# A decode kernel that reads 290 MB: rounds of two heads on halves of the partitions, with wider rows for V and the first weights

## The chip, the cores and the metric

The kernel runs on one core of one Trainium2 chip. The metric is the device time of one execution in microseconds, as the median of the runs shown. Each matmul in float32 shows as two passes on PE in the trace, each with its own weight load.

## The reference

Two rows of activations (batch B = 2, one token each, D = 448) pass through two branches, which a gate mixes:

```python
# x: (2, 1, 448); k_cache, v_cache: (2, 16, 4096, 256), all float32
g = sigmoid((x * gate_w).sum(-1, keepdims=True))
q = (x @ wq).reshape(B, Sq, 16, 256).transpose(0, 2, 1, 3)
p = softmax(einsum("bhqd,bhkd->bhqk", q, k_cache) * 256 ** -0.5)
a = einsum("bhqk,bhkd->bhqd", p, v_cache).transpose(0, 2, 1, 3).reshape(B, Sq, 4096) @ wo
h = x @ w1 + b1                      # (2, 1, 1792)
b = where(h > 0, h, 0) ** 2 @ w2 + b2
out = g * a + (1 - g) * b
```

K and V are 134 MB each; the weights wq, wo, w1 and w2 together are 21 MB. All of it is read once.

## The kernel before

**Layout.** The work goes by pairs of batch and head, 32 in all, in the order of the heads with the two batches in turn. For a pair, the 4096 keys lie on 128 partitions with 32 keys each, so that K and V are each one tile of 128 x 32 KB (4 MB, `slot`). All large tiles (K, V, wq in two, w1, w2's first two rows, w2's rest, and four groups of wo) share one pool with five slots of 32 KB per partition, the ring. A tile takes a slot when it is first written and gives it back after its last reader.

**Order.** The order of the instructions on each engine is the order in which the program writes them (`manual_schedule`). SP's queue issues all loads of the ring. An issue that waits for a slot holds up all later issues on that queue.

**One pair on the engines.** DVE multiplies K by q in place (`times_q`, L294), in three pieces of 4, 12 and 16 keys per partition for all pairs but the first. It then sums each key's 256 products (`row_sums`, L300), and takes the largest score of each partition (`maximum`, L304). PE spreads these maxima over the partitions (L306), DVE takes the largest of them with its sign changed (`softmax`, L312), and ACT writes the exponentials into a zeroed weight tile `pw` and their sums into `rs` (L317). PE multiplies the exponentials with V (`values`, L343): two keys per partition and matmul, 16 matmuls of 512 columns, in 32 passes, into four row groups of a PSUM bank. While PE and ACT do this, DVE is already at the next pair: the first 4 keys are multiplied before the exponential, the next 12 after it, and the rest in `rest`.

**Units of heads.** Four heads (two batches each) form a unit with one PSUM accumulator. When a unit is done, DVE forms the factors 1/sum times the gate (`norm`, three instructions), ACT copies the accumulator (`take`, L354), PE turns it (`turn`, L372, 16 matmuls) and multiplies it with the unit's part of wo (`project`, L385). The last four heads form units of three and one, and are projected with separate small matmuls (`late_wo`, `late_w2`, L390).

**The rest.** q for all heads is computed at the start (`project_q`, L228) from wq in two ring tiles, and is spread over the partitions for two heads at a time (`make_q`, L239). The dense branch is put in the first pairs: `load_w1` with pair 2, `ffn_hidden` and `ffn_turn` with pairs 3 and 4, the loads of w2's first two rows with pair 4, `ffn_square` (four small DVE instructions) at its end. Loads of K and V of a pair stand at L139, the loads of w2's rest at L111, of wo at L125 (units 0 to 2) and L128 (the last heads). The last pair's V is cut into pieces of 2, 1 and 1 MB; behind it, w2's rest comes in four pieces.

The last loads and the end are, in the order of the program: V of the last pair but one with wo of the last heads between its halves, V of the last pair, w2's rest; then values, the turn of the last unit, the late matmuls, one copy by ACT (L500) and two small stores.

Of the kernel before, what the change touches and what calls it, by code (L numbers as in the profile page):

```python
# [8 lines left out]
F32 = mybir.dt.float32  # L9
# [7 lines left out]
def kernel(  # L17
# [14 lines left out]
    nc = tc.nc  # L32
# [5 lines left out]
    CF = D // P  # L38
    R0 = CF * P
    RR = D - R0  # L40
    assert 2 * RR == P and B == 2 and CF == 3
    NK = S // P
    J = 32
    NCH = NK // J
# [7 lines left out]
    QH = QB // DH  # L52
    DQ = D // 4
    RING = 5
    WH = 2
    W2_CUTS = (4, 8, 11)
    LEAD = 4
# [4 lines left out]
    ring = ctx.enter_context(tc.tile_pool(name="ring", bufs=RING))  # L62
# [8 lines left out]


    wq_t = []

    def load_wq():

        ta = slot("wqa")
        nc.sync.dma_start(ta, wq[:2 * P, :].rearrange("(p c) n -> p (c n)", c=2))
# [3 lines left out]
        wq_t.extend([ta[:, :N], ta[:, N:], tb_[:, :N], tb_[:, N:N + N // 2]])  # L82

    w1_t = []

    def load_w1():
        t = slot("w1")
        nc.sync.dma_start(t[:, :2 * F], w1[:2 * P, :].rearrange("(p c) n -> p (c n)", c=2))
        nc.sync.dma_start(t[:, 2 * F:3 * F], w1[2 * P:R0, :])
        nc.sync.dma_start(t[:, 3 * F:3 * F + F // 2], w1[R0:, :].rearrange("r (s n) -> (r s) n", s=2))  # L90
        w1_t.extend([t[:, :F], t[:, F:2 * F], t[:, 2 * F:3 * F], t[:, 3 * F:3 * F + F // 2]])
# [39 lines left out]
    def load_kv(src, i, nm, cuts=(), between=None):  # L131
        b, h = pairs[i]
        v = src[b, h].rearrange("(n p j) d -> n p j d", p=P, j=J)
        tiles = []
        for n in range(NCH):
            t = slot(f"{nm}{b}_{h}_{n}").rearrange("p (j d) -> p j d", d=DH)
            at = [0, *(cuts if n == NCH - 1 else ()), J]
            for lo, hi in zip(at, at[1:]):
                nc.sync.dma_start(t[:, lo:hi, :], v[n, :, lo:hi, :])  # L139
                if between is not None and hi < J:  # L140
                    between()
            tiles.append(t)
        return tiles

    pairs = [(b, h) for h in range(H) for b in range(B)]
    last = len(pairs) - 1


    load_wq()
# [21 lines left out]
    units = [list(range(g * HG, (g + 1) * HG)) for g in range(NG - 1)] + [list(range(H - HG, H - 1)), [H - 1]]  # L171
    unit_of = {h: (u, k) for u, hs in enumerate(units) for k, h in enumerate(hs)}

    pw = {}
    for k in range(HG):
        for b in range(B):
            pw[k, b] = const.tile([P, NK // 2, 4 * HG], F32, name=f"pw{k}_{b}")
            nc.vector.memset(pw[k, b], 0.0)

# [6 lines left out]
    xr2 = const.tile([B, RR, 2], F32, name="xr2")  # L186
    nc.vector.tensor_copy(xr2, x2[:, R0:].unsqueeze(2).to_broadcast([B, RR, 2]))
    pxt = ps.tile([P, 512], F32, name="pxt", tag="sm")
    pxv = pxt[:, :(CF + 1) * B].rearrange("p (c b) -> p c b", b=B)
    for c in range(CF + 1):  # L190
        src = (x2[:, c:2 * P:2] if c < 2 else x2[:, c * P:(c + 1) * P] if c < CF
               else xr2.rearrange("b r s -> b (r s)"))
        nc.tensor.matmul(pxv[:, c, :], src, ident[:B, :B], start=True, stop=True)
    xT = const.tile([P, CF + 2, B], F32, name="xT")
    nc.vector.tensor_copy(xT[:, :CF, :], pxv[:, :CF, :])
    for s in range(2):
        nc.vector.tensor_scalar(xT[:, CF + s, :], pxv[:, CF, :], eo[:, s:s + 1], None, op0=ALU.mult)
# [19 lines left out]
    qs = const.tile([P, NQ // 4, QB], F32, name="qs")  # L217

    def project_q():
        for c in range(CF + 1):  # L220
            for n in range(NQ):
                a, gq = divmod(n, 4)
                if c < CF:
                    lt, rhs = xT[:, c, :], wq_t[c][:, n * QB:(n + 1) * QB]
                else:
                    half, m = divmod(n, NQ // 2)
                    lt, rhs = xT[:, CF + half, :], wq_t[c][:, m * QB:(m + 1) * QB]
                nc.tensor.matmul(po_bufs[a][32 * gq:32 * gq + B, :], lt, rhs, start=(c == 0), stop=(c == CF))  # L228
        for a in range(NQ // 4):
            nc.scalar.activation(qs[:, a, :], po_bufs[a], AF.Copy, scale=scale)  # L230
# [3 lines left out]
    def make_q(b, n):  # L234

        a, gq = divmod(n, 4)
        r = 32 * gq + b
        pq = ps.tile([P, 512], F32, name=f"pq{b}_{n}", tag="pq")
        nc.tensor.matmul(pq, ident[:, r:r + 1].to_broadcast([P, P]), qs[:, a, :], start=True, stop=True)  # L239
        t = work.tile([P, QB], F32, name=f"q{b}_{n}", tag=f"q{b}")  # L240
        nc.scalar.activation(t, pq, AF.Copy)  # L241
        for k in range(QH):
            q_sb[b, n * QH + k] = t[:, k * DH:(k + 1) * DH]
# [6 lines left out]
    h_sb = shared[:B, :F]  # L250

    def ffn_hidden():
        ph = ps.tile([P, 512], F32, name="ph", tag="pq")
        for c in range(CF + 1):
            for n in range(FB):
                if c < CF:
                    lt, rhs = xT[:, c, :], w1_t[c][:, n * D:(n + 1) * D]
                else:
                    half, m = divmod(n, FB // 2)
                    lt, rhs = xT[:, CF + half, :], w1_t[c][:, m * D:(m + 1) * D]  # L260
                nc.tensor.matmul(ph[32 * n:32 * n + B, :D], lt, rhs, start=(c == 0), stop=(c == CF))
        for n in range(FB):
            nc.scalar.activation(h_sb[:, n * D:(n + 1) * D], ph[32 * n:32 * n + B, :D], AF.Copy)

    def ffn_turn():
        hv = h_sb.rearrange("b (p c) -> b c p", c=FC)
        pt = ps.tile([P, FC, B], F32, name="pt", tag="sm")
        for c in range(FC):
            nc.tensor.matmul(pt[:, c, :], hv[:, c, :], ident[:B, :B], start=True, stop=True)  # L269
        return pt  # L270

    def ffn_square(pt):
        hb = const.tile([P, FC, B], F32, name="hb")
        nc.vector.tensor_tensor(hb, pt, b1T.unsqueeze(2).to_broadcast([P, FC, B]), op=ALU.add)
# [5 lines left out]
    kts, s_t, rs_t, rl_t, oT = {}, {}, {}, {}, {}  # L280

    def parts(lo, hi):

        while lo < hi:
            e = min(hi, (lo // J + 1) * J)
            yield lo // J, lo % J, lo % J + e - lo
            lo = e

    def times_q(i, lo, hi):

        b, h = pairs[i]
        for n, a, e in parts(lo, hi):
            kt = kts[i][n][:, a:e, :]
            nc.vector.tensor_tensor(kt, kt, q_sb[b, h].unsqueeze(1).to_broadcast([P, e - a, DH]), op=ALU.mult)  # L294

    def row_sums(i, lo, hi):
        if lo == 0:
            s_t[i] = work.tile([P, NK], F32, name=f"s{i}", tag="s")
        for n, a, e in parts(lo, hi):
            nc.vector.tensor_reduce(s_t[i][:, n * J + a:n * J + e], kts[i][n][:, a:e, :], axis=AX.X, op=ALU.add)  # L300

    def maximum(i):
# [3 lines left out]
        nc.tensor.matmul(mt[:, :P], m.to_broadcast([P, P]), ident, start=True, stop=True)  # L306
        return mt

    def softmax(i, mt):
        b, h = pairs[i]  # L310
        nb = work.tile([P, 1], F32, name=f"nb{i}", tag="nb")
        nc.vector.tensor_reduce(nb, mt[:, :P], axis=AX.X, op=ALU.max, negate=True)  # L312
        u, k = unit_of[h]
        c = B * k + b
        if c == 0:
            rs_t[u] = work.tile([P, B * len(units[u])], F32, name=f"rs{u}", tag="rs")
        nc.scalar.activation(pw[k, b][:, :, 2 * c:2 * c + 2], s_t[i].rearrange("p (m s) -> p m s", s=2), AF.Exp,  # L317
                             bias=nb, accum_out=rs_t[u][:, c:c + 1])

    def sums(u):  # L320
        sm = ps.tile([P, 512], F32, name=f"sum{u}", tag="sm")
        nc.tensor.matmul(sm[:, :B * len(units[u])], ones_pp, rs_t[u], start=True, stop=True)  # L322
# [12 lines left out]
    def values(i, vt, lo=0, hi=NK // 2):  # L335
        b, h = pairs[i]
        u, k = unit_of[h]
        n = len(units[u])
        po = po_bufs[u % 2]
        for m in range(lo, hi):  # L340
            r = 32 * (m % 4)
            j = 2 * m
            nc.tensor.matmul(po[r:r + 4 * n, :], pw[k, b][:, m, :4 * n],  # L343
                             vt[j // J][:, j % J:j % J + 2, :].rearrange("p j d -> p (j d)"),
                             start=(k == 0 and b == 0 and m < 4), stop=(k == n - 1 and b == B - 1 and m >= NK // 2 - 4))
# [56 lines left out]
    kts[0] = load_kv(k_cache, 0, "k")  # L402
    project_q()
    make_q(0, 0)
    make_q(1, 0)
    for n in range(NCH):
        times_q(0, n * J, (n + 1) * J)
# [123 lines left out]
```

## Time and profile before

| | us |
|---|---|
| median of 3 runs | 683.41 (683.37 to 683.63) |
| the profiled execution, device time | 683.23 |
| its span, first to last instruction | 681.4 |
| DVE busy | 581.1 |
| PE busy (matmuls) | 296.5 |
| ACT busy | 37.9 |

In the rows of the profile, a timeline line has the start, the duration, the engine, the line of the program, the operation, the output and inputs, shapes, and how many instructions were merged; in brackets stands how long the engine was idle before and what ended that. "SPq" is the issuing of a load by SP, not its transfer. In a table of stages each row has the stretch, its length, the busy time and the number of instructions of PE, PE's weight loads, DVE, ACT and GpSimd, then the granted clock of PE, the mean busy share of the 16 DMA engines and GB/s. Rows on DMA issues have the count, the size of each in KB and the median time from issue to landing.

### The profile page before, as it was taken

What the parts mean: (1) busy time and instruction counts of PE and PEld (TensorE: products, weight loads), DVE (VectorE), ACT (ScalarE), POOL (GpSimd) and SP (SyncE); (2) the same over time, 40 slices, a digit from 0 to 9 for tenths busy, and PEclk for the clock granted to TensorE, in tenths of its full rate; (3) what the DMA queues carried; (4) which work ended last, traced back from release to release, by engine and by line L of the source; (5) the groups of instructions that cost most, each with busy time, mean ns of one, the idle gap of its engine ahead of it and who ended that gap; (6) DMA issues with size and microseconds to landing.
All of it is one profiled execution on the core that took longest, in us unless ns stands there. A gap on an engine that the chain in (4) does not pass through costs nothing.

```text
span 681.4 us, 3865 instructions
## 1 busy us (share of the span) xinstructions
PE 296.5 (44%) x1598; PEld 96.8 (14%) x1598; DVE 581.1 (85%) x233; ACT 37.9 (6%) x113; POOL 0.7 (0%) x6
## 2 busy tenths in 40 slices
PE   4413445543359134433347543422455712443066
PEld 1000111400115001000014110000112200101013
DVE  3299997989896999999996999899997899999990
ACT  0200001000010000000001000000001000000000
POOL 0000000000000000000000000000000000000000
PEclk9856667787656776665667865567667757667579
DMA  8999999999999999999999999999999999999996
GB/s 370 435 433 435 430 425 431 426 434 436 431 437 430 431 431 431 430 431 431 432 426 441 431 431 432 433 429 431 431 430 423 432 431 431 430 435 437 423 419 270
DMA packets 12380, 289.79 MB, mean 425 GB/s; under 512 B 1478, under 2 KB 1612, under 8 KB 2892
## 3 DMA queue, kind: packets, MB, share of 16 engines
q1 hardware_dynamic: 12200, 289.55, 99.1%
q8 instruction: 12, 0.20, 0.1%
q10 hardware_dynamic: 164, 0.02, 0.0%
q14 instruction: 4, 0.03, 0.0%
HBM read 289.56 MB, written 0.00 MB: 425 GB/s over the span
## 4 chain that ended last, share of the span: by engine, by line
DMA 59%; DVE 37%; PE 2%; issue 0%; SPq 0%; ACT 0%; DVEq 0%; ACTq 0%
DMA k<-in_A_k_cache_dram 56%; DVE k L294 18%; DVE s L300 18%; DMA w<-in_B_w_dram 3%; PE acc L385 1%; PE po_buf L343 1%; DVE nb L312 0%; PE mt L306 0%; DVE m L304 0%; PE fin L390 0%; SPq L111 0%; ACT oT L378 0%; SPq L81 0%; ACT pw L317 0%; SPq L80 0%
## 5 line engine op out<-in xcount | busy, mean ns | idle before, releaser
L294 DVE TENSOR_TENSOR k<-k,q 128x3072 f32<-128x3072 f32 (+3 forms) x94 | 285.1, 3057 | 75.7 <-DMA k<-in_A_k_cache_dram 75.7
L300 DVE TENSOR_REDUCE s<-k 128x32 f32<-128x8192 f32 x32 | 278.0, 8686 | 2.2
L343 PE MATMUL po_buf<-v,pw 128*16 128x512 f32 (+2 forms) x1024 | 181.1, 857 | 218.3 <-DMA v<-in_A_v_cache_dram 217.4
L343 PEld LDWEIGHTS po_buf<-v,pw 128*16 128x16 f32 (+2 forms) x1024 | 36.7, 123 | 349.8 <-issue 319.7
L306 PE MATMUL mt<-ident,m 128*128 128x128 f32 x64 | 19.1, 389 | 136.2 <-DVE m L304 136.2
L317 ACT ACTIVATE pw<-s,nb 128x32 f32<-128x32 f32 x32 | 10.3, 323 | 544.0 <-DVE nb L312 544.0
L306 PEld LDWEIGHTS mt<-ident,m 128*128 128x128 f32 x64 | 11.9, 233 | 167.7 <-DVE m L304 117.1
L385 PE MATMUL acc<-wo,oT 128*2 128x448 f32 x48 | 22.9, 640 | 4.9 <-ACT oT L378 4.9
L239 PE MATMUL pq<-qs,ident 128*128 128x512 f32 x32 | 24.6, 868 | 0.0
L372 PEld LDWEIGHTS ot<-rl,shared 128*128 128x128 f32 x96 | 18.8, 304 | 0.0
L372 PE MATMUL ot<-rl,shared 128*128 128x8 f32 x96 | 18.8, 338 | 0.0
L312 DVE TENSOR_REDUCE nb<-mt 128x1 f32<-128x128 f32 x32 | 9.1, 284 | 1.7 <-PE mt L306 1.7
L241 ACT ACTIVATE q<-pq 128x512 f32<-128x512 f32 x16 | 9.4, 588 | 9.5 <-PE pq L239 9.5
L322 PE MATMUL sum<-rs,ones_pp 128*128 128x8 f32 (+2 forms) x10 | 2.8, 349 | 11.3 <-ACT pw L317 11.3
L354 ACT ACTIVATE shared<-po_buf 128x1024 f32<-128x1024 f32 x6 | 5.8, 1020 | 30.9 <-PE po_buf L343 30.9
L385 PEld LDWEIGHTS acc<-wo,oT 128*2 128x2 f32 x48 | 4.3, 94 | 21.3 <-issue 16.2
L239 PEld LDWEIGHTS pq<-qs,ident 128*128 128x128 f32 x32 | 6.9, 262 | 1.3 <-ACT qs L230 0.9
L269 PE MATMUL pt<-ident,shared 2*128 2x2 f32 x28 | 7.0, 378 | 0.0
L269 PEld LDWEIGHTS pt<-ident,shared 2*128 2x128 f32 x28 | 6.9, 336 | 0.1
L304 DVE TENSOR_REDUCE m<-s 128x1 f32<-128x32 f32 x32 | 5.9, 186 | 1.1
L317 ACT ACTIVATION_READ_ACCUMULATOR pw<-s,nb 128x1 f32 x32 | 6.0, 187 | 0.0
L228 PE MATMUL po_buf<-wqa,xT 128*2 128x512 f32 x32 | 5.6, 858 | 0.8 <-DMA wqa<-in_A_wq_dram 0.8
(62 smaller groups left out, 55.3 us busy)
## 6 DMA issues: line engine op xcount, KB each, us to landing
k<-in_A_k_cache_dram SPq DMA_DIRECT2D x32, 4096.0 KB, 40.0
v<-in_A_v_cache_dram SPq DMA_DIRECT2D x30, 4096.0 KB, 31.6
wo<-in_A_wo_dram SPq DMA_DIRECT2D x4, 1792.0 KB, 34.1
v<-in_A_v_cache_dram SPq DMA_DIRECT2D x3, 2048.0 KB, 25.9
wqa<-in_A_wq_dram SPq DMA_DIRECT2D x1, 4096.0 KB, 12.4
w<-in_B_w_dram SPq DMA_DIRECT2D x3, 896.0 KB
wqb<-in_A_wq_dram SPq DMA_DIRECT2D x1, 2048.0 KB, 16.9
v<-in_A_v_cache_dram SPq DMA_DIRECT2D x2, 1024.0 KB, 24.5
```

The source lines that it names most:

```text
L239: nc.tensor.matmul(pq, ident[:, r:r + 1].to_broadcast([P, P]), qs[:, a, :], start=True, stop=True)
L241: nc.scalar.activation(t, pq, AF.Copy)
L269: nc.tensor.matmul(pt[:, c, :], hv[:, c, :], ident[:B, :B], start=True, stop=True)
L294: nc.vector.tensor_tensor(kt, kt, q_sb[b, h].unsqueeze(1).to_broadcast([P, e - a, DH]), op=ALU.mult)
L300: nc.vector.tensor_reduce(s_t[i][:, n * J + a:n * J + e], kts[i][n][:, a:e, :], axis=AX.X, op=ALU.add)
L304: nc.vector.tensor_reduce(m, s_t[i], axis=AX.X, op=ALU.max)
L306: nc.tensor.matmul(mt[:, :P], m.to_broadcast([P, P]), ident, start=True, stop=True)
L312: nc.vector.tensor_reduce(nb, mt[:, :P], axis=AX.X, op=ALU.max, negate=True)
L317: nc.scalar.activation(pw[k, b][:, :, 2 * c:2 * c + 2], s_t[i].rearrange("p (m s) -> p m s", s=2), AF.Exp, bias=nb, accum_out=rs_t[u][:, c ...
L343: nc.tensor.matmul(po[r:r + 4 * n, :], pw[k, b][:, m, :4 * n], vt[j // J][:, j % J:j % J + 2, :].rearrange("p j d -> p (j d)"), start=(k = ...
L372: nc.tensor.matmul(ptv[:, j, :], ov[:, s, j, :], rl_t[u][:, :, s], start=(s == 0), stop=(s == 1))
L385: nc.tensor.matmul(acc[:, :D], oT[g][:, j, :], wo_sb[g][:, j, :], start=False, stop=(g == NG - 2 and j == HJ - 1))
```

## The change

Instead of one pair, a round takes two neighbouring heads of one batch: the first head's keys on partitions 0 to 63, the second's on 64 to 127, 64 keys per partition. There are 16 rounds, in the order of the head pairs with the two batches in turn.

- K of a round comes in two halves of 32 keys per partition, 4 MB each, in a ring of three slots of 32 KB, which w1, w2 and wo share as before. `load_k(i + 1, 1)` and `load_k(i + 2, 0)` are issued in round i, after V and whatever weights belong to that round.
- V of a round is one tile of 64 KB per partition, loaded with one instruction (the last one in four pieces, of 4, 2, 1 and 1 MB). It lies in a pool of its own with a single slot, `wide`. wq uses that slot first.
- wq and w1 are each loaded with one instruction, 3.5 rows of the matrix on each partition (7 half rows). x is laid out for it, with zeros where a partition holds only the other half of a row (`xT`), and `times_x` does both products. A result of q or h then lies in two groups of rows, one for each half of the columns, which `make_q`, `ffn_hidden`, `ffn_turn` and `ffn_square` take into account.
- Values of a round are 32 matmuls, 64 passes, for both heads at once: the head's partitions write their own columns of `pw`. The exponential is done with two ACT instructions, one for each half of the partitions, the spreading of the maxima and of q with two matmuls each.
- The last four heads form two units of two heads. Take, turn and projection of a unit follow directly after its last values, in the same round, not one pair later.
- w1 comes in round 1, with its product in that round; w2's first two rows come in round 3, which is also the round with wo of unit 0; wo of the last heads is loaded after V of round 14.

The core of the diff (changes to x's layout, the dense branch and the sums left out):

```diff
-    J = 32
-    NCH = NK // J
+    PH = P // 2
+    NK = S // PH
+    J = NK // 2
...
-    RING = 5
+    V_CUTS = (32, 48, 56)
...
-    ring = ctx.enter_context(tc.tile_pool(name="ring", bufs=RING))
+    ring = ctx.enter_context(tc.tile_pool(name="ring", bufs=3))
+    wide = ctx.enter_context(tc.tile_pool(name="wide", bufs=1))
...
     def load_wq():
-        ta = slot("wqa")
-        nc.sync.dma_start(ta, wq[:2 * P, :].rearrange("(p c) n -> p (c n)", c=2))
-        tb_ = slot("wqb")
-        nc.sync.dma_start(tb_[:, :N], wq[2 * P:R0, :])
-        nc.sync.dma_start(tb_[:, N:N + N // 2], wq[R0:, :].rearrange("r (s n) -> (r s) n", s=2))
+        t = wide_slot("wq")[:, :D * N // P]
+        nc.sync.dma_start(t, wq.rearrange("(r k) (s n) -> (r k s) n", k=XR, s=2).rearrange(
+            "(p k) n -> p (k n)", k=XR))
...
+    rounds = [(b, n) for n in range(H // 2) for b in range(B)]
+    def of_round(src, i):
+        b, n = rounds[i]
+        return src[b, 2 * n:2 * n + 2].rearrange("h (p j) d -> (h p) j d", p=PH)
+    def load_k(i, half):
+        t = slot(f"k{i}_{half}").rearrange("p (j d) -> p j d", d=DH)
+        nc.sync.dma_start(t, of_round(k_cache, i)[:, half * J:(half + 1) * J, :])
+        kts[i, half] = t
+    def load_v(i, cuts=()):
+        t = wide_slot(f"v{i}").rearrange("p (j d) -> p j d", d=DH)
+        at = [0, *cuts, NK]
+        for lo, hi in zip(at, at[1:]):
+            nc.sync.dma_start(t[:, lo:hi, :], of_round(v_cache, i)[:, lo:hi, :])
+        return t
...
+    def times_x(out, t, width, n):
+        for a in range(XR):
+            c, half = divmod(a, 2)
+            for g in range(n):
+                nc.tensor.matmul(out[32 * g:32 * g + 2 * B, :width], xT[:, half, c].rearrange("p s b -> p (s b)"),
+                                 t[:, (a * n + g) * width:(a * n + g + 1) * width],
+                                 start=(a == 0), stop=(a == XR - 1))
...
+    load_k(0, 0)
+    load_k(0, 1)
+    load_k(1, 0)
     project_q()
+    make_q(0)
+    make_q(1)
     def rest(i):
+        times_q(i, 0, LEAD2, J)
+        row_sums(i, 0)
+        times_q(i, 1, 0, J)
+        row_sums(i, 1)
+    times_q(0, 0, 0, LEAD2)
+    rest(0)
+    for i, (b, n) in enumerate(rounds):
+        u, k = unit_of[2 * n]
+        done = b == B - 1 and k == len(units[u]) - 2
+        vt = load_v(i, V_CUTS if i == last else ())
+        if i == 1:
+            w1_t = load_w1()
+        if i == 3:
+            load_w2_early()
+        if done and u < NG - 1:
+            load_wo(u)
         if i == last - 1:
+            load_wo(NG - 1)
         if i == last:
             load_w2_late()
         if i < last - 1:
+            load_k(i + 1, 1)
+            load_k(i + 2, 0)
+        if i == last - 2:
+            load_k(last, 1)
+        mt = maximum(i)
         if i < last:
+            times_q(i + 1, 0, 0, LEAD)
         softmax(i, mt)
         if i < last:
+            times_q(i + 1, 0, LEAD, LEAD2)
         if done:
             norm(u, sums(u))
+        if i == last:
+            break
+        values(i, vt)
+        if done:
+            take(u)
+            turn(u)
+            if u < NG - 1:
+                project(u)
+        if i == 1:
+            ffn_hidden(w1_t)
+        if i == 2:
+            pt = ffn_turn()
         if i == 3:
             for c in range(WH):
                 nc.tensor.matmul(acc[:, :D], hT[:, c, :], w2_sb[c], start=False, stop=False)
+        if i + 2 <= last:
+            make_q(i + 2)
...
+        rest(i + 1)
+        if i == 2:
             ffn_square(pt)
...
+    p1, p2, p3 = (c // 2 for c in V_CUTS)
+    values(last, vt, 0, p1)
+    values(last, vt, p1, p2)
     late_wo(H - 4)
+    values(last, vt, p2, p3)
     late_wo(H - 3)
+    values(last, vt, p3, NK // 2)
     take(NG)
-    late_wo(H - 2)
     turn(NG)
     late_w2(0, W2_CUTS[0])
+    late_wo(H - 2)
     late_wo(H - 1)
```

More of the change, by code (lines that the diff above doesn't have):

```diff
@@ L129, in load_wo @@
             wo_sb[g] = tv.rearrange("p (h j n) -> p h j n", h=HG, j=NJ)
[L131 to L149, printed above, removed]
+    rounds = [(b, n) for n in range(H // 2) for b in range(B)]
+    last = len(rounds) - 1
+    def of_round(src, i):
+        b, n = rounds[i]
+        return src[b, 2 * n:2 * n + 2].rearrange("h (p j) d -> (h p) j d", p=PH)
+    kts = {}
+    def load_k(i, half):
[7 more added lines that the diff above has]
+            nc.sync.dma_start(t[:, lo:hi, :], of_round(v_cache, i)[:, lo:hi, :])
+        return t
+    wq_t = load_wq()
     x2 = const.tile([B, D], F32, name="x2")
@@ L178 @@
             nc.vector.memset(pw[k, b], 0.0)
+    rs_t = []
+    for n in range(2):
+        rs = const.tile([P, B * HG], F32, name=f"rs{n}")
+        nc.vector.memset(rs, 0.0)
+        rs_t.append(rs)
     eo = const.tile([P, 2], F32, name="eo")
@@ L214 @@
     nc.tensor.matmul(acc[:, :D], gd[:, 1, :], b2r, start=True, stop=False)
-    qs = const.tile([P, NQ // 4, QB], F32, name="qs")
+    qs = const.tile([P, QB], F32, name="qs")
     def project_q():
[L220 to L230, printed above, removed]
@@ L232 @@
-    q_sb = {}
[L234 to L243, printed above, removed]
+        times_x(po_bufs[0], wq_t, QB, NQ // 2)
@@ new lines, in project_q, with make_q @@
+        nc.scalar.activation(qs, po_bufs[0], AF.Copy, scale=scale)
+    q_sb = {}
+    def make_q(i):
+        b, n = rounds[i]
+        a, g = divmod(n, NQ // 2)
+        r = 32 * g + B * a + b
+        pq = ps.tile([P, 512], F32, name=f"pq{i}", tag="pq")
+        for k in range(2):
+            nc.tensor.matmul(pq[k * PH:(k + 1) * PH, :DH], ident[:, r:r + 1].to_broadcast([P, PH]),
+                             qs[:, k * DH:(k + 1) * DH], start=True, stop=True)
+        q_sb[i] = work.tile([P, DH], F32, name=f"q{i}", tag=f"q{b}")
+        nc.scalar.activation(q_sb[i], pq[:, :DH], AF.Copy)
@@ L246, with ffn_hidden @@
     hT = const.tile([P, FC, B], F32, name="hT")
     shared = const.tile([P, 2 * HG * DH], F32, name="shared")
-    h_sb = shared[:B, :F]
-    def ffn_hidden():
+    h_sb = shared[:2 * B, :F]
+    def ffn_hidden(w1_t):
         ph = ps.tile([P, 512], F32, name="ph", tag="pq")
[L254 to L263, printed above, removed]
+        times_x(ph, w1_t, D, FB // 2)
+        hv = h_sb.rearrange("r (a g n) -> r g a n", a=2, n=D)
+        for g in range(FB // 2):
+            nc.scalar.activation(hv[:, g], ph[32 * g:32 * g + 2 * B, :D].unsqueeze(1).to_broadcast([2 * B, 2, D]), AF.Copy)
@@ L273, in ffn_square @@
         hb = const.tile([P, FC, B], F32, name="hb")
[L274 removed]
+        for a in range(2):
+            at = slice(a * PH, (a + 1) * PH)
+            nc.vector.tensor_tensor(hb[at], pt[at, :, a * B:(a + 1) * B], b1T[at].unsqueeze(2).to_broadcast([PH, FC, B]),
+                                    op=ALU.add)
         nc.vector.tensor_scalar(hb, hb, 0.0, None, op0=ALU.max)
```

171 lines of the change are left out of this document (50 added, 121 removed).

## The prediction

> **What bounds the kernel now.** I read the page first (engines, DMA queues, chain), then a table of stages, then the timeline at the places that the change touches.
>
> ```profile
> span 681.4 us, 3865 instructions
> PE 296.5 (44%) x1598; PEld 96.8 (14%) x1598; DVE 581.1 (85%) x233; ACT 37.9 (6%) x113; POOL 0.7 (0%) x6
> ...
> q1 hardware_dynamic: 12200, 289.55, 99.1%
> ...
> k<-in_A_k_cache_dram SPq DMA_DIRECT2D x32, 4096.0 KB, 40.0
> v<-in_A_v_cache_dram SPq DMA_DIRECT2D x30, 4096.0 KB, 31.6
> wo<-in_A_wo_dram SPq DMA_DIRECT2D x4, 1792.0 KB, 34.1
> ...
> wqa<-in_A_wq_dram SPq DMA_DIRECT2D x1, 4096.0 KB, 12.4
> ...
> w<-in_B_w_dram SPq DMA_DIRECT2D x2, 448.0 KB, 28.8
> ```
>
> SP's queue keeps all 16 DMA engines occupied for 99.1% of the span, and no compute engine is near that. Every load lies on this one queue in the order in which SP issues it, so the time is the bytes at the stream's rate plus whatever time the queue stands empty. Before, it is hardly ever empty. The stage table (the column before the last is the DMA share, the last GB/s) and two K arrivals say what the stream does:
>
> ```profile
> 266.13:305.00 38.87, 14.64 (x70) 3.66 (x70) 35.79 (x13) 1.31 (x5) 0.00 (x0) 0.60 1.00 431
> ```
> ```profile
> 267.93 1.23 DVE L294 TENSOR_TENSOR k<-k,q 128x1024 f32<-128x1024 f32 x1 [1.46 <-DMA k<-in_A_k_cache_dram]
> ...
> 287.38 1.23 DVE L294 TENSOR_TENSOR k<-k,q 128x1024 f32<-128x1024 f32 x1 [1.48 <-DMA k<-in_A_k_cache_dram]
> ```
>
> One 4 MB K and one 4 MB V arrive per 19.45 us: 9.72 us per 4 MB, 431 GB/s. DVE is busy 35.79 of 38.87 us and waits for K at each step, so it follows the stream. The change leaves the bytes alone. It can win only by making the stream denser and lose only by letting it run dry. So I ask of each load what it has to wait for, and how much is still queued when that wait ends.
>
> **How waits on buffers work here.** Three facts.
>
> ```profile
> 49.80 6.02 PE L343 MATMUL po_buf<-v,pw 128*16 128x512 f32 x32 [0.92 <-ACT pw L317]
> ...
> 55.89 0.33 SPq L139 DMA_DIRECT2D v<-in_A_v_cache_dram  x1
> ...
> 65.65 0.33 SPq L88 DMA_DIRECT2D w<-in_B_w_dram  x1
> ```
>
> First, a load takes the slot that is given back first: V2 went out at 55.89, when V0's 32 passes ended (49.80 + 6.02), and not into K1's slot, which came free at 65.65 and went to w1.
>
> ```profile
> 646.96 6.10 PE L343 MATMUL po_buf<-v,pw 128*12 128x512 f32 x32
> ...
> 653.13 3.70 SPq L111 DMA_DIRECT2D w<-in_B_w_dram  x4
> ```
>
> Second, a slot is given back whole. The first piece of w2 fills only the first 7 KB of each row, which the first passes had read early, yet it was issued at 653.13, when all 32 had ended (653.06).
>
> ```profile
> 0.74 0.39 SPq L78 DMA_DIRECT2D wqa<-in_A_wq_dram  x1
> ```
> ```profile
> 0.70:1.50 0.80, 0.00 (x0) 0.00 (x0) 0.56 (x2) 0.00 (x0) 0.50 (x2) 1.00 0.00 0
> ```
>
> Third, a load into an empty queue is slow to arrive. wqa, the first, is 4 MB like a K, and took 12.4 us from issue to landing against 9.72 in the stream: 2.7 us more. At the least it is 0.8 us (issued at 0.74, no byte before 1.50). I take 2.7, since it is this case itself, and keep 0.8 for the range.
>
> **Ordinary rounds cost nothing.** A round moves V (8 MB, 19.4 us), then two K halves (19.4 us). V of the next round needs the single wide slot, so it waits for all 64 passes of this round's values.
>
> ```profile
> 277.69 6.42 PE L343 MATMUL po_buf<-v,pw 128*16 128x512 f32 x32 [8.67 <-DMA v<-in_A_v_cache_dram]
> ...
> 297.12 5.24 PE L343 MATMUL po_buf<-v,pw 128*16 128x512 f32 x32 [10.68 <-DMA v<-in_A_v_cache_dram]
> ```
> ```profile
> 219.73 3.60 PE L343 MATMUL po_buf<-v,pw 128*16 128x512 f32 x29
> ```
>
> 32 passes from a standing start take 5.24 to 6.42 us (5.8); when PE is already running, 29 took 3.60, so the second 32 add about 3.6. The 64 take 9.4 us (8.8 to 10.0). Two K halves, 19.4 us, are still queued behind V at that time, so the next V is issued some 10 us before it is needed. The cover is those K halves; without them this wait costs what the last V pays below.
>
> K halves need a ring slot, given back by DVE:
>
> ```profile
> 30.33 8.69 DVE L294 TENSOR_TENSOR k<-k,q 128x8192 f32<-128x8192 f32 x1 [20.07 <-DMA k<-in_A_k_cache_dram]
> 39.06 8.69 DVE L300 TENSOR_REDUCE s<-k 128x32 f32<-128x8192 f32 x1
> ...
> 47.78 0.19 DVE L304 TENSOR_REDUCE m<-s 128x1 f32<-128x32 f32 x1
> ...
> 65.66 0.19 DVE L304 TENSOR_REDUCE m<-s 128x1 f32<-128x32 f32 x1
> ```
>
> A second half costs 17.4 us (30.33 to 47.75), a first half, with the maximum and the softmax of the round before in its middle, 17.9 (47.78 to 65.66). DVE has 35.3 us of work per round of 38.8, so it keeps up. Count from the landing of the first half of round i+1, when V(i) starts. The second half of round i landed 9.7 earlier and is done at 7.7; the first half of round i+1 is done at 25.6. The half of round i+2 that may need its slot comes after V and another half, at 29.1, or at 33.4 in a round with wo (1792 KB, 4.3 us): no wait. With w1 in round 1, DVE starts near 30.5 us and five halves take it to 118.5; the load that needs the slot comes at about 124. That cover is 5 us.
>
> The one load of wq makes the projection wait for all of it. DVE's first step waits for K behind wq anyway (row at 30.33), and V0, which takes wq's slot, comes 29 us later. Cost nothing, or some tenths on DVE, which has slack. The extra small operations (two exponentials, two maximum matmuls, q in two) lie on ACT and PE, at 6% and 44%.
>
> **Round 3 runs dry.** This is the round in which w2's first two rows, wo of unit 0 and two K halves are all issued, with three ring slots, one of which holds the first half of round 4. w2 and wo take the other two. Count again from V3's start: V3 lands at 19.4, w2 (448 KB, 1.1 us) at 20.5, wo at 24.8. The second half of round 4 can only have the slot of the first, free at 25.6 plus 0.5 for the three steps of the norm plus 0.7 for four steps of the square: 26.8, 2 us after the queue emptied. The first half of round 5 then needs wo's or w2's slot, and both are given back by PE only after values, take, turn and projection of unit 0. Before, the same chain:
>
> ```profile
> 195.59 6.50 PE L343 MATMUL po_buf<-v,pw 128*16 128x512 f32 x32 [5.24 <-DMA v<-in_A_v_cache_dram]
> ...
> 204.79 6.77 PE L372 MATMUL ot<-rl,shared 128*128 128x8 f32 x32
> 212.39 0.91 PE L385 MATMUL acc<-wo,oT 128*2 128x448 f32 x1 [0.82 <-ACT oT L378]
> ```
> ```profile
> 219.92 0.33 SPq L139 DMA_DIRECT2D k<-in_A_k_cache_dram  x1
> ```
> ```profile
> 673.08 1.10 PE L372 MATMUL ot<-rl,o 128*128 128x2 f32 x8 [0.34 <-ACT o L358]
> ```
>
> From the end of values (202.09) to the load that the projection releases (219.92) it took 17.8 us, of them 6.8 for the turn. At the end of the kernel, where PE had been running, 8 turns took 1.10, so 32 would take 4.4. After 64 passes PE will be running for part of it: I take 5.6 between the two, so 16.6 from the end of values. The load goes out at 19.4 + 9.4 + 16.6 = 45.4 and lands at 45.4 + 12.4 = 57.8. Without waits it would land at 24.8 + 9.7 + 9.7 = 44.2. **Cost 13.6 us**, and it contains the smaller wait before it. Everything on SP's queue stands behind it, V4 first. Bounds: values 8.8, turn 4.4, projection at its faster steps (1.5 less) and 0.8 for the restart give 8.4; values 10.0 and turn 6.8 give 15.4.
>
> **The last V runs dry.** In round 14 nothing but wo of the last heads (4.3 us) stands between V14 and V15. V14 lands at T; the 64 passes end at T + 9.4; V15's first 4 MB piece goes out then and lands at T + 21.8. Without the wait it would land at T + 4.3 + 9.7 = T + 14.0. **Cost 7.8 us** (5.3 to 8.4 with the bounds above). Behind it the order is as before: the last piece of V, then w2, and PE waits for w2 last:
>
> ```profile
> 671.32 1.04 PE L343 MATMUL po_buf<-v,pw 128*4 128x512 f32 x8 [0.68 <-DMA v<-in_A_v_cache_dram]
> ...
> 677.32 0.95 PE L390 MATMUL fin<-w,hT 128*2 128x112 f32 x32 [0.68 <-DMA w<-in_B_w_dram]
> ```
>
> The 6.0 us between them hold PE's work with 0.7 to spare; one head more after the turn adds 0.6. No cost.
>
> **What is gained: fewer packets.** V's rows of 64 KB halve its packets (4480 with the cuts become 2432), wq and w1 go from 768 to 256: 2560 fewer, 160 per engine. The queue was occupied 0.991 x 681.4 x 16 = 10,804 us of engine time. The 8064 packets of 32 KB (128 for each of the 62 whole K and V loads, and wqa) take 9808 of that at the 431 GB/s of the steady row; the other 25.3 MB at that rate take 940, and 56 are left for some 2,800 packets: 20 ns each, which is rough, since rounding 431 moves it by 4. 160 x 20 ns = 3.2 us at most; at least nothing, if a row of 64 KB travels as two packets. I take 2.0. By the Trainium skill, DMA: Bandwidth & Descriptors, Where 436 GB/s comes from, the ports carry 435 GB/s; the steady stream's distance to that is an estimate of 10 ns per packet, 1.6 us.
>
> **Sum.** The profiled execution took 683.23 us, 1.8 us over its span and 0.2 under the median of 683.41. 683.2 + 13.6 + 7.8 - 2.0 = 702.6 us, with bounds 683.2 + 8.4 + 5.3 - 3.2 = 693.7 and 683.2 + 15.4 + 8.4 = 707.0. A measurement here can tell about 0.2% (1.4 us) from no change.
>
> **The rivals.** (a) Only the last V waits. If round 3's second K half could go into a slot that isn't held by w2 or wo (the projection done early, or the early w2 load not holding a slot), the time is 683.2 + 7.8 - 2.0 = 689.0. Against it: the code puts both in the same ring. (b) Faster: slots are given back piece by piece, so that the next load follows the reader through the tile. It decides where V15's first piece is issued within 4.3 us of V14's landing; then no wait is left at either place and the time is 683.2 - 2.0 = 681.2. Against it stand the rows at 646.96 and 653.13; for it only that a new, wider tile might be treated otherwise. (c) Dearer: round 3's first waiting load is given wo's slot and not the K half's. Then it, and not the next one, goes out at 45.4 and lands at 57.8 against 34.5: 23.3 instead of 13.6, in all 712.3. Against it: the slot given back first was taken at 55.89. (d) Dearer: K is now read as 32 KB out of every 64, and neighbouring engines read addresses twice as far apart. If this slowed K's 134 MB (311 us of the stream) by 3%, 9.3 us would be added: 711.9. For it speaks nothing in this trace, where rows 32 KB apart run at 431. The Trainium skill, DMA: Bandwidth & Descriptors, Latency and other measured facts, has copies losing speed as the distance of rows grows in large powers of two, 207 against 214 GB/s at 512 KiB, a distance that no run here shows.
>
> **How the numbers follow.** Both dry spells: 0.70, 702.6, own range 693.7 to 707.0. (a) 0.10; (b) 0.10, of which 0.02 within 0.2% of before; (c) and (d) 0.10 together. Leaving out (b) and (c) with (d), 0.20, the range goes from 687.0, which holds most of (a)'s own 685.3 to 691.6, to 707.0. Faster 0.08, same 0.02, slower 0.90.
>
> **What would show it.** Right: in round 3 PE's project ends, SP issues a K load at that moment, and DVE waits longest for K just there; the GB/s row has one slice well under 400 around 195 to 220 us and another around 655 to 680; the last V's first piece is issued at the end of the 64th pass. The stream elsewhere at 431 to 434 GB/s. Wrong: no wait of DVE for K over 8 us after the start, or SP issuing the last V before values of round 14 end, or a steady rate under 428.

## The result and the profile after

| | before | after |
|---|---|---|
| median, us | 683.43 (683.37 to 683.63, 4 runs) | 703.24 (701.31 to 704.75, 4 runs) |
| profiled execution, us | 683.23 | 703.78 |
| its span, us | 681.4 | 702.0 |

The ratio is 1.0288 (95% interval 1.0261 to 1.0314): 19.8 us slower. The forecast was 702.6.

The page of the changed kernel, against the lines of before:

```profile
span 702.0 us, 3763 instructions
PE 240.4 (34%) x1618; PEld 82.8 (12%) x1618; DVE 571.9 (81%) x171; ACT 35.5 (5%) x110; POOL 0.7 (0%) x6
...
GB/s 413 399 444 422 471 418 415 429 436 450 399 311 209 418 445 448 390 451 415 474 388 434 471 395 446 420 439 428 440 437 420 441 426 433 429 426 447 300 361 275
DMA packets 9500, 289.79 MB, mean 413 GB/s; under 512 B 1158, under 2 KB 1292, under 8 KB 2316
...
q1 hardware_dynamic: 9320, 289.54, 96.2%
```

PE, DVE and ACT do less than before, and the bytes are the same, yet the queue is occupied for 96.2% of the span instead of 99.1%. The GB/s row says where: each slice is 17.55 us, and there are two holes, 311 and 209 in slices 12 and 13 (193 to 228 us) and 300 and 361 in slices 38 and 39 (649 to 684 us). Those are the two places of the forecast. The row also swings from 388 to 474 where nothing stops: a packet is put down whole to the slice in which it starts (for the same reason a share can read a little over 1 in the rows below), and a packet of 64 KB moves that sum more. Over longer stretches the stream runs as before (columns as in the table of stages: DMA share and GB/s last):

```profile
260.00:299.00 39.00, 9.13 (x64) 2.37 (x60) 35.15 (x8) 1.26 (x5) 0.00 (x0) 0.61 1.00 430
...
540.00:580.00 40.00, 21.20 (x106) 7.68 (x110) 35.15 (x8) 2.08 (x10) 0.00 (x0) 0.66 1.00 432
```

The first hole, round 3, in the timeline of the changed kernel (L345 is values, L386 the projection, L141 the load of a K half):

```profile
192.69 8.69 DVE L300 TENSOR_REDUCE s<-k 128x32 f32<-128x8192 f32 x1
...
193.77 9.26 PE L345 MATMUL po_buf<-v,pw 128*16 128x512 f32 x64 [7.66 <-DMA v<-in_A_v_cache_dram]
...
201.41 19.04 SPq L141 DMA_DIRECT2D k<-in_A_k_cache_dram  x2
...
212.56 7.53 PE L386 MATMUL acc<-wo,oT 128*2 128x448 f32 x16 [0.82 <-ACT oT L379]
213.37 8.69 DVE L295 TENSOR_TENSOR k<-k,q 128x8192 f32<-128x8192 f32 x1 [11.99 <-DMA k<-in_A_k_cache_dram]
...
232.15 1.23 DVE L295 TENSOR_TENSOR k<-k,q 128x1024 f32<-128x1024 f32 x1 [1.11 <-DMA k<-in_A_k_cache_dram]
```
```profile
198.00:201.00 3.00, 3.00 (x32) 0.80 (x28) 3.00 (x1) 0.00 (x0) 0.00 (x0) 0.96 0.03 14
...
214.00:220.00 6.00, 6.00 (x16) 1.35 (x15) 6.00 (x1) 0.00 (x0) 0.00 (x0) 0.89 0.00 0
```

From 198 to 201 us the queue is already nearly empty. SP issues the first K half at 201.41, just after DVE has summed the half whose slot it takes (192.69 + 8.69 = 201.38). The second issue, the end of that merged row, comes at 220.1, when the projection ends (212.56 + 7.53 = 220.09). From 214 to 220 us no byte moves.

The second hole, before the last V (L148 is the load of V):

```profile
659.74 8.38 PE L345 MATMUL po_buf<-v,pw 128*8 128x512 f32 x64 [20.61 <-DMA v<-in_A_v_cache_dram]
...
668.19 1.87 SPq L148 DMA_DIRECT2D v<-in_A_v_cache_dram  x4
...
680.28 6.80 PE L345 MATMUL po_buf<-v,pw 128*8 128x512 f32 x48 [4.09 <-DMA v<-in_A_v_cache_dram]
...
697.67 0.95 PE L391 MATMUL fin<-w,hT 128*2 128x112 f32 x32 [0.60 <-DMA w<-in_B_w_dram]
```

The last V goes out at 668.19, after the 64th pass on the V before it (659.74 + 8.38 = 668.12). Its first 4 MB arrive at 680.3. Behind that the end is as before: PE waits for the last piece of w2.

### The profile page after: what moved, and what is told of

The parts are those of the page before. It is cut to its first block, busy times and chain, and to the rows that moved or that the text cites. A ratio compares the mean times of both kernels' runs of the same rounds, so it can differ in the third digit from the quotient of the medians.

```text
span 702.0 us, 3763 instructions
## 1 busy us (share of the span) xinstructions
PE 240.4 (34%) x1618; PEld 82.8 (12%) x1618; DVE 571.9 (81%) x171; ACT 35.5 (5%) x110; POOL 0.7 (0%) x6
## 3 DMA queue, kind: packets, MB, share of 16 engines
q1 hardware_dynamic: 9320, 289.54, 96.2%
## 4 chain that ended last, share of the span: by engine, by line
DMA 65%; PE 20%; DVE 12%; ACT 1%; SPq 0%; issue 0%; ACTq 0%
DMA v<-in_A_v_cache_dram 59%; PE po_buf L345 17%; DVE k L295 6%; DVE s L300 6%; DMA w<-in_B_w_dram 4%; DMA wq<-in_A_wq_dram 3%; PE po_buf L215 1%; PE acc L386 1%; PE ot L373 1%; ACT shared L355 0%; SPq L148 0%; PE fin L391 0%; SPq L108 0%; ACT oT L379 0%; PE pq L252 0%
## 5 line engine op out<-in xcount | busy, mean ns | idle before, releaser
L295 DVE TENSOR_TENSOR k<-k,q 128x4096 f32<-128x4096 f32 (+3 forms) x63 | 281.7, 4487 | 95.2 <-DMA k<-in_A_k_cache_dram 76.6
L345 PE MATMUL po_buf<-v,pw 128*16 128x512 f32 (+1 forms) x1024 | 145.5, 730 | 166.1 <-DMA v<-in_A_v_cache_dram 166.1
L308 PE MATMUL mt<-ident,m 128*64 128x64 f32 x64 | 7.7, 335 | 256.4 <-DVE m L304 256.4
L345 PEld LDWEIGHTS po_buf<-v,pw 128*16 128x16 f32 (+1 forms) x1024 | 32.2, 110 | 265.7 <-issue 225.3
L319 ACT ACTIVATE pw<-s,nb 64x64 f32<-64x64 f32 x32 | 11.2, 349 | 295.6 <-DVE nb L314 295.2
L386 PE MATMUL acc<-wo,oT 128*2 128x448 f32 x48 | 24.3, 671 | 2.5 <-ACT oT L379 2.5
L255 ACT ACTIVATE q<-pq 128x256 f32<-128x256 f32 x16 | 6.1, 384 | 209.9 <-PE pq L252 209.8
L252 PE MATMUL pq<-qs,ident 128*64 128x256 f32 x64 | 10.7, 419 | 0.7 <-ACT qs L241 0.7
L215 PE MATMUL po_buf<-wq,xT 128*4 128x512 f32 x56 | 8.1, 741 | 4.7 <-DMA wq<-in_A_wq_dram 4.7
L276 PEld LDWEIGHTS pt<-ident,shared 4*128 4x128 f32 x28 | 6.9, 336 | 0.9 <-issue 0.9
L276 PE MATMUL pt<-ident,shared 4*128 4x4 f32 x28 | 7.0, 380 | 0.0
L386 PEld LDWEIGHTS acc<-wo,oT 128*2 128x2 f32 x48 | 4.4, 97 | 20.1 <-issue 17.3
```

The costliest lines, as they stand in the source:

```text
L215: nc.tensor.matmul(out[32 * g:32 * g + 2 * B, :width], xT[:, half, c].rearrange("p s b -> p (s b)"), t[:, (a * n + g) * width:(a * n + g + ...
L252: nc.tensor.matmul(pq[k * PH:(k + 1) * PH, :DH], ident[:, r:r + 1].to_broadcast([P, PH]), qs[:, k * DH:(k + 1) * DH], start=True, stop=True)
L255: nc.scalar.activation(q_sb[i], pq[:, :DH], AF.Copy)
L276: nc.tensor.matmul(pt[:, c, :], hv[:, c, :], ident[:2 * B, :2 * B], start=True, stop=True)
L295: nc.vector.tensor_tensor(kt, kt, q_sb[i].unsqueeze(1).to_broadcast([P, hi - lo, DH]), op=ALU.mult)
L308: nc.tensor.matmul(mt[at, :PH], m.to_broadcast([P, PH]), ident[:, at], start=True, stop=True)
```

## The experiments

The theory was that of the forecast: two dry spells of the queue, 13.6 and 7.8 us, less some 2 us for fewer packets. The rivals were that the new layout slows the stream everywhere, and other causes of the wait in each place. The runs lie on several chips; the kernel before, measured again beside each of them, had medians of 683.29 to 683.47 us.

**Round 3 without its crowding.** w2's first rows and their product go to round 4:

```diff
-        if i == 3:
+        if i == 4:
             load_w2_early()
...
-        if i == 3:
+        if i == 4:
             for c in range(WH):
```

> w2's first two rows are loaded, and multiplied, one round later (round 4 instead of 3); nothing else. Theory (two dry spells): in round 3 the first half of round 5 can then take the slot of the first half of round 4, which DVE gives back 7 us before it is needed, so the wait of DVE for K of 12 us in round 3 goes: 703.2 - 13.6 = 689.6 us. Rival (the wider stride of K and the two-head layout slow the stream as a whole, and the dry spell is made up for elsewhere): within 2 us of 703. Rival (wo alone is enough to hold up round 3): 698 or more.

Measured: 690.57 us (689.83 to 692.23), 12.7 less. wo by itself doesn't hold up the round, and the layout doesn't carry that loss. DVE still waits for K in this round, but for 6.3 us and not for 12.0, which is wo's own share of the stream and an ordinary round's wait.

**Only the later of the two waits.** The product with w2's first rows goes ahead of the take:

```diff
         values(i, vt)
+        if i == 3:
+            for c in range(WH):
+                nc.tensor.matmul(acc[:, :D], hT[:, c, :], w2_sb[c], start=False, stop=False)
...
-        if i == 3:
-            for c in range(WH):
-                nc.tensor.matmul(acc[:, :D], hT[:, c, :], w2_sb[c], start=False, stop=False)
```

> In round 3 the product with w2's first two rows comes before the take, the turn and the projection of unit 0, and not after them; loads as in the changed kernel. Theory: w2's slot is given back at about 31 us after V3's start instead of 46, before the first waiting K half (issued at 27, landing at 39) has landed; of the 13.6 us only that first wait, 4 to 5 us, is left: 703.2 - 9 = 694 us. Rival (wo's slot is the one that is waited for, whatever w2 does): no change. Rival (no wait is left at all): 689.6.

Measured: 696.05 us (695.34 to 696.24), 7.2 less, where 9 was expected. Its round 3:

```profile
193.89 8.44 PE L345 MATMUL po_buf<-v,pw 128*16 128x512 f32 x64 [7.81 <-DMA v<-in_A_v_cache_dram]
201.38 2.80 SPq L141 DMA_DIRECT2D k<-in_A_k_cache_dram  x2
202.16 1.67 PE L453 MATMUL acc<-w,hT 128*2 128x448 f32 x4
...
213.55 8.69 DVE L295 TENSOR_TENSOR k<-k,q 128x8192 f32<-128x8192 f32 x1 [12.20 <-DMA k<-in_A_k_cache_dram]
```

The second K half now goes out at 203.8, right after that product (202.16 + 1.67), while the first is still on its way. Only the wait for DVE's half is left: it lands at 213.5 and, by the working of the forecast, would have landed 15.1 after V3 (4.3 for wo, 9.7 for the half and 1.1 for w2), at 209.0. That is 4.5 us; the difference to the kernel without either wait is 5.5. So the 13.6 us were two waits in a row, and the cheap part of the cure is the order on PE.

**More of the suspected work.** The turn of unit 0 is done twice:

```diff
+            if u == 0:
+                turn(u)
             turn(u)
```

> The turn of unit 0 is done twice in round 3 (the same result twice). Theory: that turn is part of PE's chain which sets when the next K half goes out, so its 6.6 us and the copies behind it, 7 to 8 us, appear in full: 710.5 us. Rival (the wait is set by DVE or by the landing of wo): no change.

Measured: 712.65 us (710.66 to 713.59), 9.4 more. The turn's 32 further passes took 6.4 us in the profile, and the K half behind the projection arrived 7.9 us later (240.0 against 232.15); the rest is within the scatter of both kernels. Work on PE, which is busy for a third of the time, shows in full here.

**The last V without its wait.** Its first half goes into a ring slot and is issued ahead of wo (the lines that keep `load_v` from loading that half again are left out):

```diff
         if i == last - 1:
+            va = slot("va").rearrange("p (j d) -> p j d", d=DH)
+            nc.sync.dma_start(va, of_round(v_cache, last)[:, :J, :])
             load_wo(NG - 1)
...
-    values(last, vt, 0, p1)
+    values(last, va, 0, p1)
```

> The first half of the last V goes into a ring slot, right behind the V before it; the rest into the wide slot. Nothing else. Theory: the dry spell before the last V goes, 6.5 to 7.8 us: 703.2 - 7 = 696 us, with round 3 as it was. Rival (PE is late at the end anyway, with all of the last values to do): under 3 us gained.

Measured: 697.46 us (695.45 to 698.00), 5.8 less. PE was not late at the end: its last product still waits for w2 there, 0.59 us.

**Both together.**

> w2's first two rows one round later, and the first half of the last V in a ring slot of its own, issued right behind the V before it, so that it doesn't wait for the wide slot. Theory: no dry spell is left, the fewer packets remain: 683.4 - 2.0 = 681.4 us, faster than the kernel before by 0.3%, and the scatter from run to run falls from 3 us to some tenths, as PE's chains no longer set the end. Rival (stride or layout): 690 or more, or a steady stream under 428 GB/s.

Measured: 682.49 us (681.88 to 683.94, 11 runs), ratio 0.9987 (0.9978 to 0.9996): faster than the kernel before by 1.0 us, and 20.8 faster than the change as it stood. Its queue:

```profile
q1 hardware_dynamic: 9320, 289.54, 99.0%
```
```profile
266.13:305.00 38.87, 9.72 (x72) 2.66 (x72) 34.76 (x9) 1.26 (x5) 0.00 (x0) 0.63 1.00 430
```

With the two-head layout, K's wider stride and the wide rows all in place, the stream runs at 430 GB/s where it ran at 431 in the same stretch before. So the two holes are the whole loss. The expectation was wrong in two sizes: the gain is 1.0 (0.3 to 1.5 by the interval) and not 2.0, and the scatter fell only from 3.4 to 2.1 us; before, it is 0.5. Part of the first is seen at the end of the profile, where PE's last product has no wait for w2 in front of it any more:

```profile
675.12 1.72 PE L392 MATMUL fin<-w,hT 128*2 128x112 f32 x64
```

The last piece of w2 landed at 676.2 here and at 677.8 before, 1.7 us earlier, but the span ended only 1.2 us earlier: the last steps of DVE and PE, and not the stream, set the end in this execution. Whether the scatter comes from them too was not tested.

**The price of a packet.** V in two or four loads of narrower rows (the last V as it was):

```diff
-        at = [0, *cuts, NK]
+        at = [0, *cuts, NK] if cuts else list(range(0, NK + 1, NK // 2))
```

> As the kernel with both mends, but each V in two loads of 32 KB rows into the same tile (the last V as it was). Theory: one packet more per partition and V, 8 per engine and round at about 11 ns, 15 rounds: 1.3 us more than with 64 KB rows, 682.7. Rival (a 64 KB row travels as two packets anyway): no difference. Rival (the gain came from fewer loads, not wider rows): also slower, but then four loads cost three times as much as two, whatever the rows.

> As the kernel with both mends, but each V in four loads of 16 KB rows. Theory (a price for each packet): 24 packets more per engine and round, 15 rounds, 11 ns: 4.0 us more than with 64 KB rows, 685.4. Rival (no price for packets): no difference.

Measured on the same chip: 682.49 with 64 KB rows, 683.37 (682.96 to 684.19) with 32 KB, 685.33 (685.05 to 686.57) with 16 KB. That is 0.9 us for 120 packets more per engine and 2.8 for 360: 7 to 8 ns each. These times alone can't tell packets from loads, since both grew in the same proportion (one and three loads more for each V, eight and 24 packets).

The trace can, because it keeps the duration of every packet: the median is 2420 ns for 64 KB, 1215 for 32 KB and 613 for 16 KB. Two packets of 32 KB take 10 ns longer than one of 64, and four of 16 KB take 32 ns longer, so 10 to 11 ns for each further packet, whatever the loads. A further load adds only 16 short packets of 9 ns, one for each engine. The landing of the last piece of w2 agrees: it came at 676.2, 677.6 and 680.0 us in the three profiles, 1.4 and 3.8 us later for 135 and 405 packets per engine with the short ones. The time of the kernel shows less of it, in part because its end does not always wait for that landing.

A 64 KB row doesn't travel as two packets: the trace of the kernel with both mends has 1920 packets of 65,536 bytes, 128 for each of the 15 whole V.

**The cover of the ordinary wait.** All these start from the kernel with both mends. In six rounds PE multiplies V again into a scratch bank that nobody reads, so that V's slot is held longer:

```diff
         values(i, vt)
+        if i in (5, 6, 8, 9, 10, 12):
+            pd = ps.tile([P, 512], F32, name=f"pd{i}", tag="sm")
+            for m in range(32):
+                nc.tensor.matmul(pd[:4 * HG, :], pw[k, b][:, m % 32, :], vt[:, 2 * (m % 32):2 * (m % 32) + 2, :].rearrange("p j d -> p (j d)"),
+                                 start=True, stop=True)
```

> As the kernel with both mends, and in six rounds (5, 6, 8, 9, 10, 12) PE multiplies V another 32 times (64 passes) into a scratch bank that nobody reads, so that V's slot is held 7 to 9 us longer. It measures the cover of the wait for the wide slot in ordinary rounds. Theory: the next V is issued some 9 us before the queue would run empty (19.4 us of K halves, less 9.4 for the values and 0.8 for the issue), so that 7 to 9 us more just fit: no change from 682.5, at most 2. Rival (there is no such cover, each round already waits for the values): 6 times 7 to 9, some 45 us more.

> The same with 64 more multiplications (128 passes, some 14 to 15 us) in the same six rounds. Theory: the cover is exceeded by 5 to 6 us in each of them, and the restart adds up to 2: 6 times 5 to 8 = 30 to 48 us, some 720. Rival (the stream doesn't depend on PE at all): 682.5.

Measured: 802.06 and 967.46 us, both far outside. The reason is in the length of the extra passes, which I had taken from the values:

```profile
277.18 9.11 PE L346 MATMUL po_buf<-v,pw 128*16 128x512 f32 x64 [10.88 <-DMA v<-in_A_v_cache_dram]
286.10 27.63 PE L457 MATMUL pd<-v,pw 128*16 128x512 f32 x64
```

64 passes took 27.63 us, not 7, because they all write one row group of the bank, while values rotate over four. With the hold as it really was, the terms of the forecast fit: hold after the landing, less 19.4 for the K halves, plus 2.7 for the restart. 36.7 (9.1 + 27.6) - 19.4 + 2.7 = 20.0, times six 120.0 (measured 119.6 over 682.49); 64.4, with the extra passes counted twice, gives 47.7, times six 286 (measured 285.0). The runs were repeated with the passes spread over the groups, `pd[32 * (m % 4):32 * (m % 4) + 4 * HG, :]`:

> The 64 extra passes in the same six rounds now go to the four row groups in turn, as the values themselves do, and not all to one. In the run with one group a pass took 0.43 us and 64 of them 27.6 us, four times as long as in the values. Theory: spread, they take about 7 us, V's slot is held for 16 us after V's landing, the queue lasts 19.4, and the next load must be issued about 1 us earlier: no change from 682.5, at most 2 us. Rival (no cover): 6 times 7, 724.

> 128 extra passes in the same six rounds, over four row groups in turn: about 14 us. Theory, as the two runs on one group follow it (hold after the landing less 19.4 plus 2.7 for the restart, six times: 36.7 gave 119.6, 64.4 gave 285.0): 9.1 + 13.8 - 19.4 + 2.7 = 6.2, six times 37: 719.7 us. Rival (still covered): 682.5.

> 32 extra passes in the same six rounds, over four row groups in turn: 3.5 us, so that V's slot is held for 12.6 us after the landing. The run with 64 lost 5.6 us in all where none was expected. Theory: the landing is that of the slowest of the 16 DMA engines; the fastest is 2 to 3 us ahead and runs out of K 16.7 us after that landing, and the issue takes 1 us, so the cover is 15.7 and not 18.6 us; 16 to 16.2 exceeded it a little in each round, 12.6 does not: no change from 682.5, at most 0.7. Rival (the extra passes cost PE or the stream something by themselves): half of 5.6, 685.3.

Measured: 688.13 (688.05 to 688.75) with 64 passes, 720.19 (718.57 to 721.54) with 128, 682.66 (682.27 to 682.86) with 32. The longest hold came out as forecast, the shortest cost nothing, and the middle one cost 5.6 us where none was forecast. In the profiles the holds were 12.0 to 13.1 us with 32 passes and 15.2 to 16.6 with 64; of the latter the shortest lost nothing and the other five about 1 us each, as shown below. So the cover ends a little over 15 us after a landing and not at 18.6.

The reason I gave for it, that the 16 DMA engines don't finish a load together, is seen where the queue runs dry. This is the kernel with only the last V's wait, with wo as the last load before the hole:

```profile
645.00:646.00 1.00, 0.18 (x4) 0.15 (x8) 1.00 (x1) 0.00 (x0) 0.00 (x0) 0.50 1.03 409
...
647.00:648.00 1.00, 1.00 (x8) 0.17 (x4) 1.00 (x1) 0.00 (x0) 0.00 (x0) 0.50 0.60 237
...
649.00:650.00 1.00, 1.00 (x16) 0.32 (x12) 1.00 (x1) 0.00 (x0) 0.00 (x0) 1.00 0.06 25
650.00:651.00 1.00, 1.00 (x16) 0.21 (x8) 0.97 (x2) 0.00 (x0) 0.00 (x0) 1.00 0.00 0
```

The mean share falls from full to nothing over more than 3 us. The traces show it for every load too, since they keep 16 completions of each, as many as there are engines. In the kernel with both mends the first completion of a load comes 1.0 us before the last at 40 us of the span, 1.7 before it from 80 to 257 us, 2.6 from 408 to 519 and 3.3 at 645. So the engines drift apart while the stream runs. Where the queue runs dry they come together again: in the changed kernel the distance is 1.7 us before the hole of round 3 and 0.3 behind it.

In the run with 64 extra passes the distance is 2.2 to 2.8 us in the six rounds, so the first engine is out of work that much before the landing by which I had counted. From the first completion of the last K half to that of the next V it takes 19.4 us in every round without extra passes. It took the same in round 5, where that V was issued 2.3 us before the first engine had done the K half, and 20.3 to 20.6 in the other five, where it was issued only 0.7 to 1.4 us before. That is 1.0 to 1.3 us in each of the five, 5.7 in all, against 5.6 by the medians. So the missing 3 us are the lead of the first engine, and an issue that has to come somewhere between 1.4 and 2.3 us before that engine's end, where I had counted 0.8.

## Why the prediction was right

**The bound.** The stream at 431 GB/s set the time before and sets it after, outside the two holes. Right, by the rows of both kernels and of the kernel with both mends, where only the end follows DVE and PE.

**Round 3.** The forecast counted from V3's start, with its landing at 19.4 and the late K half at 57.8, that is 38.4 later. In the profile the values of V3 began at 193.77 and DVE's work on that half at 232.15: 38.4. Against 24.8 without waits the cost is 13.6, as forecast. The parts were nearly as exact: values 9.3 (9.4 forecast), take to projection's end 17.0 (16.6), issue to landing 12.0 (12.4). Leaving the cause out gave 12.7 us, and 15.0 with the last V's wait also gone (697.46 - 682.49).

**The last V.** Forecast 7.8. In the profile its first piece landed 20.5 us after the V before it, against 14.0 without a wait: 6.5. Leaving it out gave 5.8, and 8.1 with round 3 mended (690.57 - 682.49). These two, like the pair above, differ by 2.3 us, which the medians of four runs with 2 to 3 us of scatter can't settle; by the profiles' spans the same pairs give 8.3 and 7.8, and 14.0 and 13.5. Values took 8.4 us here, not 9.4, and less than the 8.8 that I had put as the least. Their length depends on when the clock steps up:

```profile
659.00:660.00 1.00, 0.26 (x4) 0.15 (x8) 1.00 (x1) 0.00 (x0) 0.00 (x0) 0.50 1.03 412
...
663.00:664.00 1.00, 1.00 (x12) 0.21 (x8) 1.00 (x1) 0.00 (x0) 0.00 (x0) 1.00 0.18 72
```

The passes begin at a granted clock of 0.50 and go on at 1.00 from about 662.5, at 12 instead of 8 a microsecond and more. When that step comes varies: the turn in round 3 took 6.57 us in the changed kernel and 3.59 with w2 moved, though it is the same code. Here PE's chain sets the time, so that moment moves the length of the round: in the profile of the kernel with only the last V mended, whose round 3 is the same program, the turn took 3.89 us and the late K half went out 24.5 us after V3's landing instead of 26.3. This may be what spreads 701 to 705, and the pairs above; no run tested that.

**The gain.** The count was right (2880 packets fewer, of which 2560 carry data, as forecast); the price was not. I took 2.0 us, between 20 ns a packet and nothing; the packets' own durations show 10 to 11 ns, 1.7 us for 160 packets, and of that the time of the kernel shows 1.0. This is the term that was sized wrong, because the 20 ns came from a small difference of two large products. By the Trainium skill, DMA: Bandwidth & Descriptors, Where 436 GB/s comes from, the distance to the port ceiling had given 10 ns as an estimate (worked out again from 435 and 431 GB/s it is 11). The trace agrees with that, with its 10 to 11, and not with my rows.

**The sum.** 702.6 against 703.24 is closer than its terms. The last V was taken 1.3 us too dear and the gain 1.0 us too large, which nearly cancel, and the four runs alone spread over 3.4 us. That closeness is luck; the two holes, their places and their causes are not.

**Ordinary rounds.** Free, as forecast, but with less in hand: a hold of 15.2 us was still free and one of 15.4 was not, so that about 6 us are left beside values of 9.4, where I had counted some 10. The step that was too generous is the one that took a landing for the moment at which all engines stand; the first of them stands 1.7 to 3.3 us sooner.

**The rivals.** (a) fell: both waits were there. (b) fell: SP issued the last V at 668.19, after the last pass at 668.12, so a slot of the wide pool is given back whole too. (c) fell: the first late K half went out at 201.41, into DVE's slot. (d) fell: K read as 32 KB out of every 64 leaves the stream at 430 to 432 GB/s. The loss at a row distance of 512 KiB, which the prediction took from the Trainium skill, DMA: Bandwidth & Descriptors, Latency and other measured facts, isn't touched by these runs.

## What to carry to other kernels

In a kernel that one queue of loads bounds, ask of each load what it waits for and how many bytes lie queued when that wait ends. PE, busy for 34% of the time, cost 13 to 15 us here and a slot that DVE held some 5, at the only two points where the queue was shorter than the chain that gives back a slot. Rounds with extra loads and the last round are the places to look, and the cure was to move a small load to a round with room and to give the last load another slot. Count the cover to the end of the first DMA engine, which came 1.7 to 3.3 us before the landing in the running stream, with some 2 us for the issue, and the price of an empty queue with the restart, 12 us for 4 MB instead of 9.7.

## What the runs showed of the hardware that was not expected

Matmuls with 16 output rows that write the four row groups of a bank in turn run four at a time: 64 passes of 512 columns took 7.05 us in turn and 27.63 us on one group, a factor of 3.9, both at a granted clock of 1.00. In turn, four passes begin within 0.02 us of one another every 0.43 us; on one group, a single pass begins every 0.43 us.

```profile
285.08 7.05 PE L457 MATMUL pd<-v,pw 128*16 128x512 f32 x64
```

The Trainium skill, TensorEngine Tiling (Array Packing), Key Properties, has such tiles working independently of each other, and its Theoretical Speedup up to 4 times for outputs of at most 32 rows; the trace agrees with its 3.9. What was new to me is that the values owe three quarters of their speed to it, and that an added probe loses it when it writes to one place.
